# MHA decode with a ReGLU block: an eighth of the last query-weight row is loaded into the first 24 partitions by six short transfers

## The chip, the cores and the metric

One Trainium2 chip, one of its NeuronCores. The metric is the device time of one execution in microseconds (us). The core has 16 DMA engines that bring data from HBM into the on-chip memory of 128 partitions, and five compute engines: PE (TensorE), DVE (VectorE), ACT (ScalarE), POOL (GpSimd) and SP (SyncE, which here only issues transfers).

## What is computed

One token of a decoder layer. The reference, cut to what matters:

```python
def _A_ref(x, k_cache, v_cache, wq, wo):          # H, Dh = 32, 192; Sk = 8192; D = 640
    q = (x @ wq).reshape(B, Sq, H, Dh).transpose(0, 2, 1, 3)
    scores = jnp.einsum("bhqd,bhkd->bhqk", q, k_cache) * (Dh ** -0.5)
    p = _softmax(scores, axis=-1)
    o = jnp.einsum("bhqk,bhkd->bhqd", p, v_cache)
    return o.transpose(0, 2, 1, 3).reshape(B, Sq, H * Dh) @ wo

h  = x + _A_ref(_layernorm(x), k_cache, v_cache, wq, wo)
h2 = h + _B_ref(_layernorm(h), W_gate, W_up, W_down)   # (relu(gate) * up) @ W_down
```

All is in 32-bit floats. The two caches are 32 heads x 6 MB each; wq is 640 x 6144, which is 15 MB.

## The kernel before, in words

Everything large comes through one queue, the one that SP issues, and in the order of the program. A transfer of 128 rows fills one row in each partition.

**The query weights (L69 to L75).** Partition p holds the five rows 5p to 5p+4 of wq, 24 KB each. Three transfers bring them: rows 0 and 1 of each partition (6 MB, one tile of the pool `kv`), rows 2 and 3 (6 MB, the second tile), and row 4, the last (3 MB, half of the third tile). The pool `kv` has three such tiles and no more, so the loads of the caches take them over in turn: the first K load (head 0) waits until PE has done with rows 0 and 1, the second K load waits for rows 2 and 3, and the first V load for the last row.

**The queries (L154 to L164).** `xT` (x spread over the partitions, five values each) and `xrow` (x as one row) come on ACT's own queue, `xT` as 128 rows and `xrow` as a single row. After the layer norm, `xn` holds five normed values per partition, and for each j of 0 to 4 PE multiplies `xn[:, j]` with the weights' row j: 12 matmuls of 512 columns, three banks `qp0` to `qp2` by four groups of 32 output partitions. ACT copies the banks to `q4`, and `query(h)` (L168) spreads a pair of heads over all partitions.

**The heads (L292 to L310).** For each head SP loads K of the next head and V of this one, 6 MB each (48 KB a partition). DVE multiplies K by the query and sums (L188, L193) with POOL's help (L189), a softmax follows, and PE multiplies by V (L228). The rows of `wo` come in groups between them (L91).

**The end (L318 to L382).** The ReGLU weights take over two tiles of `kv`. Of W_down, twelve rows a partition, the last three come as transfers of one row each (L332), and the last four steps are: the last row of W_down lands, PE's last eight passes (L378), one DVE instruction (L381), the store of 640 results.

**Completion semaphores.** Each transfer adds to one of eight semaphores that the framework hands out in turn (DMAHW0 to DMAHW7 below). A transfer that is given a semaphore which an earlier transfer used waits on SP until that earlier one has landed.

The profile's line numbers are those of this listing.

Of the kernel before, what the change touches and what calls it, by code (L numbers as in the profile page):

```python
# [7 lines left out]
F32 = mybir.dt.float32  # L8
AF = mybir.ActivationFunctionType
ALU = mybir.AluOpType  # L10
AX = mybir.AxisListType
# [3 lines left out]
def kernel(  # L15
# [12 lines left out]
    nc = tc.nc  # L28
    P, Q, NQ = 128, 32, 4
    _, H, S, DH = kc.shape  # L30
    D = wq.shape[0]
    F = w_gate.shape[1]
    DJ = D // P
# [4 lines left out]
    TW = R * DH  # L38
    HPQ = H // NQ
    QB = 512  # L40
    NQB = HPQ * DH // QB
# [10 lines left out]
    const = ctx.enter_context(tc.tile_pool(name="const", bufs=1))  # L52
    kv = ctx.enter_context(tc.tile_pool(name="kv", bufs=3))
# [6 lines left out]
    ps_s = ctx.enter_context(tc.tile_pool(name="ps_s", bufs=2, space=bass.MemoryType.PSUM))  # L60
# [5 lines left out]
    nc.scalar.dma_start(xrow, x[0])  # L66


    wq_v = wq.rearrange("(p j) n -> p j n", p=P)  # L69
    wq_ts = []  # L70
    for j in range(0, DJ, 2):
        n = min(2, DJ - j)
        t3 = kv.tile([P, 2 * TW], F32, name="kv_t").rearrange("p (j n) -> p j n", n=TW)[:, 0:n, :]
        nc.sync.dma_start(t3, wq_v[:, j:j + n, :])
        wq_ts += [t3[:, i, :] for i in range(n)]  # L75

    def load_kv(src, h, parts):
        t = kv.tile([P, 2 * TW], F32, name="kv_t")
# [19 lines left out]
    ident = const.tile([P, P], F32, name="ident")  # L98
# [45 lines left out]
    xn = const.tile([P, DJ], F32, name="xn")  # L144
# [4 lines left out]
    for g in range(NQ):  # L149
        nc.tensor.matmul(acc[g * Q:(g + 1) * Q, :], ones[0:1, 0:Q], xrow[:, g * DG:(g + 1) * DG],  # L150
                         start=True, stop=False)


    qps = [ps_q.tile([P, QB], F32, tag="q", name=f"qp{b}") for b in range(2)]  # L154
    qps.append(ps_x.tile([P, QB], F32, tag="x", name="qp2"))
    for j in range(DJ):
        for b in range(NQB):
            for g in range(NQ):
                c0 = g * HPQ * DH + b * QB
                nc.tensor.matmul(qps[b][g * Q:(g + 1) * Q, :], xn[:, j:j + 1].to_broadcast([P, Q]),  # L160
                                 wq_ts[j][:, c0:c0 + QB], start=(j == 0), stop=(j == DJ - 1))
    q4 = const.tile([P, HPQ * DH], F32, name="q4")
    for b in range(NQB):
        nc.scalar.copy(q4[:, b * QB:(b + 1) * QB], qps[b])  # L164
# [129 lines left out]
    for h in range(H):  # L294
        gi, i = group_of[h]
# [80 lines left out]
    for j in range(FJ):  # L376
        for g in range(NQ):
            nc.tensor.matmul(pd[g * Q:(g + 1) * Q, 0:DG], guT[:, j, :], dn[:, j, g * DG:(g + 1) * DG],  # L378
                             start=(j == 0), stop=(j == FJ - 1))
# [30 lines left out]
```

## Time and profile before

| what | value |
|---|---|
| time, median of 3 runs | 1045.59 us (1045.57 to 1045.64) |
| time of the profiled execution | 1045.79 us |
| its span, first to last instruction | 1044.0 us |
| bytes moved in it | 446.35 MB, 428 GB/s over the span |
| busy: PE / DVE / POOL / ACT | 37% / 64% / 42% / 5% of the span |
| chain that ended last, by engine | DMA 62%, DVE 25%, PE 9%, issue 4% |

The span leaves out 1.8 us that lie around the instructions. "DMA share" in the rows below is the time that the packets which started in a stretch took, over 16 engines and the length of that stretch; it can exceed 1.00 by a little in a short stretch, since a packet counts where it started. One packet is one row of a transfer, or the word of 4 bytes that raises the semaphore. Engine busy times are in us, with the number of instructions in brackets.

### The profile page before, as it was taken

The numbers are of one execution on the slowest core, as the hardware profiler recorded it, in microseconds if no ns is written. First come the engines' busy times: TensorE is split into PE (matmuls) and PEld (weight loads), VectorE is DVE, ScalarE is ACT, GpSimd is POOL, SyncE is SP. The second block draws the span as 40 slices with busy tenths as digits, with TensorE's granted clock in tenths as the row PEclk, the third lists the DMA queues.
The fourth block names the chain that finished last, engine by engine and source line by source line (L and its number), as shares of the span: only waits on it lengthen the run. The fifth ranks groups of instructions, "written<-read, shape, count | busy, mean of one in ns | idle before, by whom it ended". The sixth has DMA issues, their size and how long they took to land.

```text
span 1044.0 us, 6866 instructions
## 1 busy us (share of the span) xinstructions
PE 391.3 (37%) x2872; PEld 126.6 (12%) x2872; DVE 666.6 (64%) x419; ACT 47.2 (5%) x141; POOL 440.2 (42%) x139
## 2 busy tenths in 40 slices
PE   1603343343345223344433333353323434341375
PEld 0101111011011011111110111011111111110122
DVE  1086777566667766567775666677665667766551
ACT  0000000000000000000000000000000000000010
POOL 0055555344455544245553444455542455544330
PEclk9856656666666566676656666665666666666678
DMA  9999999999999999999999999999999999999997
GB/s 396 441 427 431 430 439 430 429 430 441 424 432 433 436 426 428 440 434 429 434 432 432 429 436 433 432 428 436 433 420 443 434 430 431 432 432 427 433 422 297
DMA packets 13000, 446.35 MB, mean 428 GB/s; under 512 B 1573, under 2 KB 1577, under 8 KB 3114
## 3 DMA queue, kind: packets, MB, share of 16 engines
q1 hardware_dynamic: 12824, 445.92, 99.2%
q8 instruction: 22, 0.36, 0.1%
q14 instruction: 8, 0.07, 0.0%
q10 hardware_dynamic: 146, 0.01, 0.0%
HBM read 445.91 MB, written 0.00 MB: 427 GB/s over the span
## 4 chain that ended last, share of the span: by engine, by line
DMA 62%; DVE 25%; PE 9%; issue 4%; SPq 0%; ACTq 0%; ACT 0%; DVEq 0%
DMA kv_t<-in_A_k_cache_dram 57%; DVE kv_t L188 19%; PE po L228 6%; DVE sc L193 4%; DMA xrow<-in_A_x_dram 2%; DMA ffn_b<-in_B_W_down_dram 2%; DMA ffn_a<-in_B_W_up_dram 2%; PE q L173 2%; PE qp L160 1%; DVE oT L272 1%; DVE m L203 0%; DVE rl L213 0%; DVE mp L198 0%; SPq L82 0%; SPq L91 0%
## 5 line engine op out<-in xcount | busy, mean ns | idle before, releaser
L189 POOL TENSOR_TENSOR kv_t<-kv_t 128x1536 f32<-128x1536 f32 x128 | 438.3, 3447 | 559.8 <-DVE mp L198 254.6
L188 DVE TENSOR_TENSOR kv_t<-kv_t,q 128x3072 f32<-128x3072 f32 x128 | 427.5, 3343 | 300.6 <-DMA kv_t<-in_A_k_cache_dram 290.1
L228 PE MATMUL po<-kv_t,p 128*2 128x384 f32 x2048 | 215.3, 581 | 99.1 <-DMA kv_t<-in_A_v_cache_dram 99.0
L193 DVE TENSOR_REDUCE sc<-kv_t 128x16 f32<-128x1536 f32 x128 | 215.0, 1740 | 0.0
L200 PE MATMUL ps_small<-ident,mp 128*128 128x128 f32 x64 | 24.3, 483 | 399.3 <-DVE mp L198 399.3
L228 PEld LDWEIGHTS po<-kv_t,p 128*2 128x2 f32 x2048 | 53.7, 95 | 252.3 <-issue 147.9
L200 PEld LDWEIGHTS ps_small<-ident,mp 128*128 128x128 f32 x64 | 15.8, 307 | 421.3 <-issue 375.7
L268 PE MATMUL ps_small<-ob,par 128*32 128x192 f32 (+1 forms) x144 | 44.5, 479 | 0.7 <-ACT ob L231 0.7
L173 PE MATMUL q<-q,sel 128*128 128x384 f32 x32 | 21.3, 765 | 54.5 <-DVE kv_t L188 54.5
L231 ACT ACTIVATE ob<-po,rl 128x384 f32<-128x384 f32 x32 | 18.6, 581 | 437.9 <-PE po L228 437.9
L246 PE MATMUL acc<-wo_t,oT 128*3 128x480 f32 x112 | 32.9, 902 | 11.2 <-DVE oT L272 11.2
L210 PE MATMUL ps_small<-rs,ones 128*128 128x1 f32 x64 | 18.6, 359 | 48.1 <-ACT p L208 48.1
L205 ACT ACTIVATE nb<-m 128x1 f32<-128x1 f32 x32 | 6.5, 203 | 484.6 <-DVE m L203 484.4
L210 PEld LDWEIGHTS ps_small<-rs,ones 128*128 128x128 f32 x64 | 15.8, 308 | 74.6 <-ACT p L208 62.9
L268 PEld LDWEIGHTS ps_small<-ob,par 128*32 128x32 f32 x144 | 16.7, 154 | 16.1 <-issue 6.7
L160 PE MATMUL qp<-kv_t,xn 128*32 128x512 f32 x120 | 16.5, 705 | 3.9 <-DMA kv_t<-in_A_wq_dram 2.9
L272 DVE STREAM_TRANSPOSE oT<-ps_small 32x192 f32<-32x192 f32 (+1 forms) x32 | 11.6, 364 | 8.8 <-PE ps_small L268 8.1
L173 PEld LDWEIGHTS q<-q,sel 128*128 128x128 f32 x32 | 6.7, 258 | 63.8 <-DVE kv_t L188 49.6
L238 DVE MEMSET acc<- 128x512 f32 x1 | 0.5, 485 | 20.0 <-ACT q L164 20.0
L208 ACT ACTIVATE p<-sc,nb 128x64 f32<-128x64 f32 x32 | 11.2, 349 | 1.0
L127 DVE TENSOR_REDUCE s<-xT 128x1 f32<-128x5 f32 x1 | 0.2, 159 | 17.1 <-DMA xT<-in_A_x_dram 17.1
L203 DVE TENSOR_REDUCE m<-ps_small 128x1 f32<-128x128 f32 x32 | 9.1, 285 | 2.2 <-PE ps_small L200 2.2
(76 smaller groups left out, 76.5 us busy)
## 6 DMA issues: line engine op xcount, KB each, us to landing
kv_t<-in_A_k_cache_dram SPq DMA_DIRECT2D x32, 6144.0 KB, 37.0
kv_t<-in_A_v_cache_dram SPq DMA_DIRECT2D x31, 6144.0 KB, 23.1
wo_t<-in_A_wo_dram SPq DMA_DIRECT2D x7, 1920.0 KB, 27.0
kv_t<-in_A_wq_dram SPq DMA_DIRECT2D x2, 6144.0 KB, 18.1
ffn_a<-in_B_W_up_dram SPq DMA_DIRECT2D x1, 3840.0 KB
kv_t<-in_A_wq_dram SPq DMA_DIRECT2D x1, 3072.0 KB, 39.2
kv_t<-in_A_v_cache_dram SPq DMA_DIRECT2D x1, 3072.0 KB, 31.9
kv_t<-in_A_v_cache_dram SPq DMA_DIRECT2D x4, 768.0 KB, 35.5
```

The lines of the kernel that those rows point to most:

```text
L160: nc.tensor.matmul(qps[b][g * Q:(g + 1) * Q, :], xn[:, j:j + 1].to_broadcast([P, Q]), wq_ts[j][:, c0:c0 + QB], start=(j == 0), stop=(j == ...
L173: nc.tensor.matmul(q[:, 0:2 * DH], sel[:, g, :], q4[:, i * DH:(i + 2) * DH], start=True, stop=True)
L188: keep(nc.vector.tensor_mul(ks, ks, q[:, None, :].to_broadcast([P, SUB, DH])))
L189: nc.gpsimd.tensor_add(ks[:, :, 0:HD], ks[:, :, 0:HD], ks[:, :, HD:DH])
L193: keep(nc.vector.reduce_sum(sc[:, i0:i0 + SUB], ks[:, :, 0:HD], axis=AX.X))
L200: keep(nc.tensor.matmul(pt[:, 0:P], mp.to_broadcast([P, P]), ident, start=True, stop=True))
L210: nc.tensor.matmul(pl[:, 0:1], ones, rs, start=True, stop=True)
L228: nc.tensor.matmul(po[g * Q:g * Q + 2, :], p[:, 2 * i:2 * i + 2], vt[:, 2 * i * DH:(2 * i + 2) * DH], start=(i < NQ), stop=(i >= NP - NQ))
L231: nc.scalar.activation(ob, po, AF.Copy, scale=rl)
L246: nc.tensor.matmul(acc3[g * Q:g * Q + 3, 0:W3], oT[:, t:t + 3, 0], w3[:, g * W3:(g + 1) * W3], start=(gi == 0 and t == 0), stop=(gi == LAS ...
L268: nc.tensor.matmul(pt[q0:q0 + Q, 0:W], par[:, k, :], ob[:, k * DH + u * W:k * DH + (u + 1) * W], start=(k == 0), stop=(k == 1))
L272: keep(nc.vector.transpose(oT[s], pt[s, 0:W].rearrange("p (c j) -> p j c", c=Q)))
```

## The change

The last row of each partition is cut at column 5376. Its first 5376 columns come as before, in one transfer of 128 rows of 21 KB. The other 768 columns (3 KB), an eighth of the row, don't go to their own partition any more: the 128 pieces are put into the first 24 partitions, in six slots of 3 KB side by side. Slot s of 0 to 4 takes 24 pieces, those of the partitions 8s to 8s+7, 40+8s to 40+8s+7 and 80+8s to 80+8s+7; the last slot takes the eight pieces of the partitions 120 to 127. These six transfers stand ahead of that of the 5376 columns.

Since the pieces now lie in other partitions, the normed x values that belong to them must lie there too: `to_x` and `in_x` are two patterns of ones and zeros, made from the identity, and a matmul with them puts the 128 values of `xn[:, 4]` into `xx`, 24 partitions by six slots. PE then takes the 768 columns from the six slots: 12 matmuls with 24 (the last slot: 8) rows, added to the same banks.

```diff
     wq_ts = []
-    for j in range(0, DJ, 2):
-        n = min(2, DJ - j)
-        t3 = kv.tile([P, 2 * TW], F32, name="kv_t").rearrange("p (j n) -> p j n", n=TW)[:, 0:n, :]
-        nc.sync.dma_start(t3, wq_v[:, j:j + n, :])
-        wq_ts += [t3[:, i, :] for i in range(n)]
+    for j in range(0, DJ - 1, 2):
+        t3 = kv.tile([P, 2 * TW], F32, name="kv_t").rearrange("p (j n) -> p j n", n=TW)
+        nc.sync.dma_start(t3, wq_v[:, j:j + 2, :])
+        wq_ts += [t3[:, i, :] for i in range(2)]
+    t3 = kv.tile([P, 2 * TW], F32, name="kv_t")
+    wq_x = t3[:, TW:TW + SX * NX].rearrange("p (s n) -> p s n", n=NX)
+    wq_l = wq_v[:, DJ - 1, CX:TW]
+    wq_a = wq_l[0:5 * PX].rearrange("(a s b) n -> a b s n", a=3, b=8)
+    for s in range(SX - 1):
+        nc.sync.dma_start(wq_x[0:PX, s, :], wq_a[:, :, s, :])
+    nc.sync.dma_start(wq_x[0:8, SX - 1, :], wq_l[5 * PX:P])
+    nc.sync.dma_start(t3[:, 0:CX], wq_v[:, DJ - 1, 0:CX])
+    wq_ts.append(t3[:, 0:TW])
...
+    to_x = const.tile([P, PX], F32, name="to_x")
+    id_x = ident[:, 0:5 * PX]
+    nc.vector.reduce_sum(to_x.rearrange("p (a b) -> p a b", a=3), id_x.rearrange("p (a s b) -> p a b s", a=3, b=8),
+                         axis=AX.X)
+    nc.vector.tensor_add(to_x[:, 0:8], to_x[:, 0:8], ident[:, 5 * PX:P])
+    in_x = const.tile([P, SX], F32, name="in_x")
+    nc.vector.reduce_sum(in_x[:, 0:SX - 1], id_x.rearrange("p (a s b) -> p s a b", a=3, b=8), axis=AX.XY)
+    nc.vector.reduce_sum(in_x[:, SX - 1:SX], ident[:, 5 * PX:P], axis=AX.X)
+    xs = const.tile([P, SX], F32, name="xs")
+    nc.vector.tensor_scalar_mul(xs, in_x, xn[:, DJ - 1:DJ])
+    px = ps_s.tile([P, 512], F32, name="ps_small")
+    nc.tensor.matmul(px[0:PX, 0:SX], to_x, xs, start=True, stop=True)
+    xx = const.tile([PX, SX], F32, name="xx")
+    nc.vector.tensor_copy(xx, px[0:PX, 0:SX])
...
+    for s in range(SX):
+        k = PX if s < SX - 1 else 8
+        for b in range(NQB):
+            c1 = (NQ - 1) * HPQ * DH + (b + 1) * QB
+            c0 = max(c1 - QB, CX)
+            if c0 < c1:
+                query_part(b, NQ - 1, c0, c1, xx[0:k, s:s + 1].to_broadcast([k, Q]),
+                           wq_x[0:k, s, c0 - CX:c1 - CX], False, s == SX - 1)
```

Here CX = 5376, NX = 768, PX = 24 and SX = 6; `query_part` is the matmul of L160 with its columns given.

On SP's queue, at the program's start, the transfers stood so before (L74 the query weights, L82 the caches, L91 the rows of `wo`):

```order
L74 DMA kv_t<-in_A_wq_dram 128x12288 x2
L74 DMA kv_t<-in_A_wq_dram 128x6144
L82 DMA kv_t<-in_A_k_cache_dram 128x12288 [waits DMAHW1_49,PE_49]
L91 DMA wo_t<-in_A_wo_dram 128x3840
L82 DMA kv_t<-in_A_k_cache_dram 128x12288 [waits DMAHW3_49,PE_49]
L82 DMA kv_t<-in_A_v_cache_dram 128x12288 [waits DMAHW4_49,DMAHW0_49,PE_49]
```

and now so (L76, L83 to L85 the query weights, L93 the caches, L102 `wo`):

```order
L76 DMA kv_t<-in_A_wq_dram 128x12288 x2
L83 DMA kv_t<-in_A_wq_dram 24x1x768 x4
L83 DMA kv_t<-in_A_wq_dram 24x1x768 [waits DMAHW0_49]
L84 DMA kv_t<-in_A_wq_dram 8x768 [waits DMAHW1_49]
L85 DMA kv_t<-in_A_wq_dram 128x5376 [waits DMAHW2_49]
L93 DMA kv_t<-in_A_k_cache_dram 128x12288 [waits DMAHW3_49,PE_49]
L102 DMA wo_t<-in_A_wo_dram 128x3840 [waits DMAHW4_49]
L93 DMA kv_t<-in_A_k_cache_dram 128x12288 [waits DMAHW5_49,PE_49]
```

There are four transfers more, and the eight semaphores now go round once within the query weights: the fifth short transfer waits for `xT` (DMAHW0), the sixth for rows 0 and 1 of the weights (DMAHW1), the long rest for `xrow` (DMAHW2), and the first K load for rows 2 and 3 (DMAHW3).

On PE, the matmuls of the weights' last row stood so before (`qp_149` to `qp_151` are the three banks):

```order
L160 MATMUL qp_149<-kv_t,xn 32x512 [waits DMAHW4_49]
L160 MATMUL qp_149<-kv_t,xn 32x512 x3
L160 MATMUL qp_150<-kv_t,xn 32x512 x4
L160 MATMUL qp_151<-kv_t,xn 32x512 x4
L173 MATMUL q<-q_212,sel 128x384 [waits Activation_49,Pool_49]
```

and now so:

```order
L185 MATMUL qp_167<-kv_t,xn 32x512 [waits DMAHW2_49]
L185 MATMUL qp_167<-kv_t,xn 32x512 x3
L185 MATMUL qp_168<-kv_t,xn 32x512 x3
L185 MATMUL qp_168<-kv_t,xn 32x256
L185 MATMUL qp_169<-kv_t,xn 32x512 x3
L185 MATMUL qp_168<-kv_t,xx 32x256 [waits DMAHW4_49,DVE_49]
L185 MATMUL qp_169<-kv_t,xx 32x512
L185 MATMUL qp_168<-kv_t,xx 32x256 [waits DMAHW5_49]
```

The twelve matmuls became 11 and then six pairs (two pairs' beginnings are shown), each pair waiting for its own short transfer. The matmul with `to_x` (L176) stands ahead of the first matmul of the weights.

## Rows read from the trace of the kernel before

**Rows 1.** the page's part 3: queue, kind: packets, MB, share of 16 engines' span
```profile
q1 hardware_dynamic: 12824, 445.92, 99.2%
q8 instruction: 22, 0.36, 0.1%
```

**Rows 2.** busy time by stretch: engines, granted PE clock, DMA share, GB/s
```profile
60.00:400.00 340.00, 121.61 (x832) 38.35 (x832) 241.29 (x138) 14.77 (x45) 163.31 (x48) 0.62 1.00 432
400.00:1000.00 600.00, 219.17 (x1544) 70.58 (x1548) 407.96 (x238) 24.50 (x80) 273.31 (x80) 0.63 1.00 431
```

**Rows 3.** the chain that ended last, 1000 to 1044: start us, us, what
```profile
1021.66 18.58 DMA ffn_b<-in_B_W_down_dram
1040.28 0.52 PE pd L378 x8
1040.83 0.38 DVE o L381
```

**Rows 4.** busy time by stretch, the last 7 us of the transfers
```profile
1033.00:1034.00 1.00, 0.00 (x0) 0.00 (x0) 0.94 (x2) 0.00 (x0) 0.00 (x0) 1.00 1.01 405
1034.00:1034.50 0.50, 0.47 (x16) 0.45 (x20) 0.00 (x0) 0.00 (x0) 0.00 (x0) 1.00 0.96 389
1034.50:1035.00 0.50, 0.50 (x18) 0.22 (x8) 0.00 (x0) 0.00 (x0) 0.00 (x0) 1.00 0.65 266
1035.50:1036.00 0.50, 0.46 (x16) 0.44 (x20) 0.00 (x0) 0.00 (x0) 0.00 (x0) 1.00 0.53 215
1037.00:1038.00 1.00, 0.13 (x4) 0.13 (x8) 0.00 (x0) 0.00 (x0) 0.00 (x0) 1.00 0.52 202
1039.00:1039.50 0.50, 0.18 (x10) 0.01 (x2) 0.00 (x0) 0.00 (x0) 0.00 (x0) 1.00 0.12 46
1039.70:1039.90 0.20, 0.20 (x8) 0.00 (x0) 0.00 (x0) 0.00 (x0) 0.00 (x0) 1.00 0.04 13
```

**Rows 5.** DMA packets that start between 1.7 and 3.1 us
```profile
DMA packets 16, 0.79 MB, mean 562 GB/s; under 512 B 0, under 2 KB 0, under 8 KB 0
```

**Rows 6.** queue 10's packets in 18.4 to 18.5, 18.98 to 19, 20.89 to 20.9
```profile
q10 hardware_dynamic: 2, 0.00, 1.1%
...
q10 hardware_dynamic: 1, 0.00, 31.9%
...
q10 hardware_dynamic: 1, 0.00, 5.6%
```

**Rows 7.** DMA packets that start between 115.6 and 115.7 us, by queue
```profile
q8 instruction: 1, 0.02, 68.4%
```

**Rows 8.** DMA issues (KB each, median us to landing), then the timeline (start us, us)
```profile
ffn_b<-in_B_W_down_dram SPq DMA_DIRECT2D x3, 320.0 KB, 27.5
...
1039.49 0.48 PE L378 MATMUL pd<-ffn_b,guT 128*32 128x160 f32 x8 [0.32 <-DMA ffn_b<-in_B_W_down_dram]
1040.28 0.48 PE L378 MATMUL pd<-ffn_b,guT 128*32 128x160 f32 x8 [0.31 <-DMA ffn_b<-in_B_W_down_dram]
```

**Rows 9.** timeline of the front: start us, us, what [idle before <-releaser]
```profile
19.03 0.16 DVE L127 TENSOR_REDUCE s<-xT 128x1 f32<-128x5 f32 x1 [17.15 <-DMA xT<-in_A_x_dram]
21.33 0.74 PE L150 MATMUL acc<-xrow,ones 1*32 1x160 f32 x2 [1.50 <-DMA xrow<-in_A_x_dram]
31.02 0.33 SPq L82 DMA_DIRECT2D kv_t<-in_A_k_cache_dram  x1
33.41 7.05 PE L160 MATMUL qp<-kv_t,xn 128*32 128x512 f32 x48 [2.46 <-DMA kv_t<-in_A_wq_dram]
40.94 2.78 PE L160 MATMUL qp<-kv_t,xn 128*32 128x512 f32 x24 [0.48 <-DMA kv_t<-in_A_wq_dram]
43.78 0.33 SPq L82 DMA_DIRECT2D kv_t<-in_A_v_cache_dram  x1
55.58 13.15 DVE L188 TENSOR_TENSOR kv_t<-kv_t,q 128x3072 f32<-128x3072 f32 x4 [10.54 <-DMA kv_t<-in_A_k_cache_dram]
```

**Rows 10.** all 68 cache loads (L82): issue to landing
```profile
DMA to landing us min/median/max: 22.8/33.4/45.3
```

More of the change, by code (lines that the diff above doesn't have):

```diff
@@ L69 @@
     wq_v = wq.rearrange("(p j) n -> p j n", p=P)
+    CX, NX, PX, SX = TW - 768, 768, 24, 6
     wq_ts = []
-    for j in range(0, DJ, 2):
-        n = min(2, DJ - j)
-        t3 = kv.tile([P, 2 * TW], F32, name="kv_t").rearrange("p (j n) -> p j n", n=TW)[:, 0:n, :]
-        nc.sync.dma_start(t3, wq_v[:, j:j + n, :])
-        wq_ts += [t3[:, i, :] for i in range(n)]
+    for j in range(0, DJ - 1, 2):
[11 more added lines that the diff above has]
+    wq_ts.append(t3[:, 0:TW])
     def load_kv(src, h, parts):
@@ L151, with query_part @@
                          start=True, stop=False)
+    to_x = const.tile([P, PX], F32, name="to_x")
[12 more added lines that the diff above has]
+    nc.vector.tensor_copy(xx, px[0:PX, 0:SX])
     qps = [ps_q.tile([P, QB], F32, tag="q", name=f"qp{b}") for b in range(2)]
     qps.append(ps_x.tile([P, QB], F32, tag="x", name="qp2"))
+    def query_part(b, g, c0, c1, lhs, w, start, stop):
+        d = g * HPQ * DH + b * QB
+        nc.tensor.matmul(qps[b][g * Q:(g + 1) * Q, c0 - d:c1 - d], lhs, w, start=start, stop=stop)
     for j in range(DJ):
@@ L159 @@
                 c0 = g * HPQ * DH + b * QB
-                nc.tensor.matmul(qps[b][g * Q:(g + 1) * Q, :], xn[:, j:j + 1].to_broadcast([P, Q]),
-                                 wq_ts[j][:, c0:c0 + QB], start=(j == 0), stop=(j == DJ - 1))
+                c1 = c0 + QB
+                last = j == DJ - 1
+                moved = last and c1 > CX
+                if moved:
+                    c1 = max(c0, CX)
+                if c0 < c1:
+                    query_part(b, g, c0, c1, xn[:, j:j + 1].to_broadcast([P, Q]), wq_ts[j][:, c0:c1],
+                               j == 0, last and not moved)
+    for s in range(SX):
[3 more added lines that the diff above has]
+            c0 = max(c1 - QB, CX)
+            if c0 < c1:
+                query_part(b, NQ - 1, c0, c1, xx[0:k, s:s + 1].to_broadcast([k, Q]),
+                           wq_x[0:k, s, c0 - CX:c1 - CX], False, s == SX - 1)
     q4 = const.tile([P, HPQ * DH], F32, name="q4")
```

## The prediction, made before the changed kernel ran

> **What bounds the kernel now.** I read the queues first, then the stretches, then the chain's end, then the last microseconds one half at a time.
>
> SP's queue holds nearly all the bytes, and its packets fill 99.2% of 16 engines' span [rows 1]. In the two long stretches that hold 940 us the DMA share is 1.00, at 431 to 432 GB/s [rows 2]. So the 16 engines never wait for an issue there, and one engine moves 432 / 16 = 27.0 GB/s. Compute runs beside this; what waits for DMA in the middle is not what to shorten. The chain's end says the same: the last landing of W_down, then 0.52 us of PE, then 0.38 us of DVE, and the store [rows 3]. The time ends when the slowest engine has moved its share.
>
> The engines don't finish together [rows 4]. Until 1034 the share is 1.01. These last rows have packets of 2.5 KB, at which a busy engine shows about 0.95 of its time, so the share times 16 / 0.95 counts the engines still at work: 11 from 1034.5 to 1035 (0.65), 9 from 1035.5 on (0.53 and, two us later, 0.52), 2 from 1039 (0.12), and less than one from 1039.7 (0.04). Five engines stop near 1034.4, two more near 1035.3, nine go on, and the last one stops near 1039.8. So seven engines are ahead of the last: five by some 5.4 us, two by some 4.5 us. Bytes moved from the late engines to those seven shorten the kernel; bytes moved the other way lengthen it.
>
> What makes engines unequal is seen in part. A packet of the instruction queue took 0.684 x 0.1 x 16 = 1.09 us of one engine [rows 7], and there are 22 [rows 1]; dealt to nine engines that is 2.7 us each, near the gap between the two groups.
>
> **What the change moves.** Each 128-row transfer puts eight rows on each engine: the first 16 packets are one row of 48 KB for each of 16 engines (0.79 MB) [rows 5]. The change takes 3 KB from each of 128 rows, on every engine 8 x 3,072 = 24,576 bytes, which at 27.0 GB/s is **-0.91 us on each of the 16**.
>
> What it adds depends on how 24 rows are dealt, which no row shows. The ends are: even over all 16 (0.91 us come back, nothing moved) and all on one engine (128 packets there). The nearest rows are the 128-row transfers with eight rows an engine, so I take eight an engine: 24 rows are three engines, in five transfers, and the last eight rows fall one to an engine on eight. An engine of the three gets 5 x 8 + 1 = 41 packets of 3 KB. Price of one: the 2.5 KB rows of W_down land 0.79 us apart for a 320 KB transfer [rows 8], eight packets an engine, so 0.099 us each, and by size 0.119 us for 3 KB. That is 41 x 0.119 = 4.9 us, and net **+4.0 us on three engines**; five others get one packet, **-0.8 us**; eight keep **-0.91 us**. With all 128 on one engine it would be 128 x 0.119 - 0.91 = +14.3 us there.
>
> [...]
>
> Which three? A single row goes to one engine, and `xrow` was that: its packet started at 18.98 to 19.00, its semaphore word at 20.89 to 20.90 [rows 6], one 48 KB packet (1.82 us at 27.0 GB/s) behind it. So its engine had ended its part of `xT` at 18.98 - 1.82 = 17.2, while the last engine did so between 18.4 and 18.5 [rows 6]. I take a short transfer to begin on that same engine: it is 1.3 us ahead at the start. Its two neighbours are not seen. If all three are among the five that lead by 5.4 us, they end 1.4 us ahead of the old end, the late ones 0.91 ahead, and the gain is full. If one is among the two with 4.5 us, it ends 0.5 ahead, and that is the gain.
>
> **What else it touches, and what covers it.** SP's fifth short transfer waits for `xT` (19.03), the sixth for rows 0 and 1, the rest for `xrow` (21.3) [rows 9]. Rows 2 and 3 are in the queue until 33.4 [rows 9], so 12 us cover these waits. The first K load moves from 31.02 to some 33.5 (it now waits for rows 2 and 3); the rest still in the queue is 8 x 21,504 bytes an engine, 6.4 us, which covers it. The six small DVE instructions and one matmul stand ahead of PE's first weights: at 0.16 us [rows 9] to 0.25 us each, at most 2 us, before a wait that ends at 33.41 anyway. PE's last row was 24 passes in 2.78 us [rows 9], 0.116 each; now it is 46, at most 5.3 us, and begins up to 4 us later: the first V load moves from 43.78 to 50 at most, with two loads and `wo` ahead of it (33 us of queue). Queries are ready near 51, K lands at 55.5 [rows 9] or up to 3 us later on the loaded engines. Then buffers come free 3 us later; the shortest load took 22.8 us from issue to landing [rows 10], and itself needs 6,144 KB / 432 GB/s = 14.6 us, so 8 us of older work stood before it. All nothing on the path; if the cover failed, the loss would be what an engine idles.
>
> **Sum.** -0.91 us at the late engines, the three loaded ones just below: -0.3 to -0.91, and I take -0.8. The profiled execution, 1045.79 us, would give 1045.0; its span of 1044.0 and the 1.8 us around it otherwise stay. It lies 0.2 us over the median 1045.59, so I forecast **1044.8 us**, range of this case 1044.6 to 1045.3. That is under 0.1%, and 0.2% (2.1 us) is about what a measurement of this kernel can tell from no change.
>
> **Rivals.**
> - *One of the three is a late engine.* The nine late ones lead the last by 0 to some 2.5 us, since nine are still at work after 1037 [rows 4]. With +4.0 us on it the end moves by +1.5 to +4.0 us: 1047.1 to 1049.6, **slower**. It decides when a loaded engine leads the last by less than 4.0 us. For it: nine of 16 are late, and only one of the three is seen, only at the start. Against it: that one is ahead, and the late group is explained by instruction packets, which I would expect to be dealt to a fixed part of the engines, more likely a run of neighbours than a scatter. Chance 0.15.
> - *The 24 rows are spread over more engines.* Then nothing is moved and 41 small packets become 8 to 11 an engine: 8 x 0.119 - 0.91 = +0.04 us, **1045.6 us**. [...] For it: 128 rows do so; against: 24 is no multiple of 16. Chance 0.06.
> - *The front runs dry* through the new waits on SP. The loads then start late and every engine idles alike; up to 1 us, **1046.3 us**. The 12 and 6.4 us of cover speak against it. Chance 0.03.
> - *Faster by over 0.2%* needs 2.1 us, more than the 0.91 us that leave a late engine; only another dealing of instruction packets could add it. Chance 0.02.
>
> The forecast keeps 0.74. Within 0.2% lie the forecast, the spread, most of the dry front and the mildest of the late engine: 0.84. Slower by over 0.2%: 0.13. Faster: 0.03. For eight in ten the range must hold the forecast, the spread and the dry front: 1044.4 to 1046.4 us, 0.83.
>
> **What would show it.** In the changed profile: the queue's packets grow by 128 rows and 23 semaphore words (three for each of five transfers, eight for the sixth); in the last microseconds fewer engines stop at 1034, since three of the seven now go on to about 1038.5, and the last stops near 1038.9; the share stays 1.00 in the long stretches. Wrong would be: a share that falls to one or two engines for several us at the end (a late engine was loaded), or seven engines that still stop at 1033.5 (nothing was moved).

## The result, and the profile after

The changed kernel took **1050.82 us** (median of six runs, 1048.17 to 1051.55), beside 1045.62 us (1045.41 to 1045.9) for the kernel before on the same chip: ratio 1.0043, 95% interval 1.003 to 1.0056. It is slower by 5.2 us, outside the range that was given. The profiled execution took 1050.48 us, with a span of 1048.6 us. Four of the six runs took 1050.5 to 1051.6 us and two 1048.2 and 1048.4; what is read below is a profile of the first kind, and no view tells why two runs were spared some 2.5 us, which is about what the late query is found to cost below.

The queues come first: the page's part 3 of the changed kernel, to be laid beside [rows 1].

```profile
q1 hardware_dynamic: 12975, 445.92, 99.1%
q8 instruction: 23, 0.38, 0.1%
```

The bytes are the same, and SP's queue has 151 packets more: 128 short rows and 23 semaphore words, which is three for each of five transfers and eight for the sixth. Of the 146 packets on ACT's queue 129 are the rows of `xT` and `xrow` and 17 such words, one of them for the single row of `xrow` [rows 6] and so 16 for the 128 rows of `xT`; three words are then three engines. The 24 rows were dealt as predicted, and the fault is not there.

Next the stretches. This is the busy time by stretch in the front of the changed kernel, with the columns of [rows 2]; DMA share and GB/s are the last two.

```profile
32.00:34.00 2.00, 1.12 (x12) 0.29 (x12) 0.00 (x0) 0.00 (x0) 0.00 (x0) 1.00 1.07 330
34.00:36.00 2.00, 2.00 (x24) 0.65 (x20) 0.00 (x0) 0.00 (x0) 0.00 (x0) 1.00 1.09 296
36.00:38.00 2.00, 2.00 (x24) 0.52 (x16) 0.00 (x0) 0.00 (x0) 0.00 (x0) 1.00 0.84 230
38.00:40.00 2.00, 0.48 (x8) 0.00 (x0) 0.00 (x0) 0.00 (x0) 0.00 (x0) 1.00 1.08 328
40.00:42.00 2.00, 0.00 (x0) 0.00 (x0) 0.00 (x0) 0.00 (x0) 0.00 (x0) 0.98 1.09 467
```

Read the last two columns together. The share stays near 1.0, so the engines are busy; yet they move 230 to 330 GB/s where the long stretches have 432 [rows 2]. A packet simply takes longer: the trace's rows of 21.5 KB that started from 34 to 38 us took 1.13 to 1.42 us each, those from 42 us on 0.80 to 0.81. The stretch is the one in which the short transfers are in flight, and at 40 us, when they are done, the rate is back.

The timeline of the front, to be laid beside [rows 9]:

```profile
33.16 0.33 SPq L93 DMA_DIRECT2D kv_t<-in_A_k_cache_dram  x1
...
46.64 5.34 PE L185 MATMUL qp<-kv_t,xn 128*32 128x512 f32 x22 [8.16 <-DMA kv_t<-in_A_wq_dram]
...
51.91 12.21 PE L185 MATMUL qp<-kv_t,xx 24*32 24x256 f32 x24
...
64.14 0.33 SPq L93 DMA_DIRECT2D kv_t<-in_A_v_cache_dram  x1
...
65.73 13.15 DVE L233 TENSOR_TENSOR kv_t<-kv_t,q 128x3072 f32<-128x3072 f32 x4 [0.33 <-PE q L218]
```

PE waits 8.16 us for the last row, which lands at 46.6 and not at 40.9. Then come the 24 passes on the short rows: 12.21 us, 0.51 us each. They are not alike, since the 768 columns of a slot fall into a piece of 256 and one of 512; the groups of instructions from 46 to 66 us, forms kept apart, show it for the first five slots (busy us, then mean ns of one):

```profile
L185 PE MATMUL qp<-kv_t,xx 24*32 24x512 f32 x10 | 7.2, 811 | 0.0
L185 PE MATMUL qp<-kv_t,xx 24*32 24x256 f32 x10 | 4.0, 489 | 0.0
```

The first V load is issued at 64.14 (43.78 before), and what releases DVE is now the query (PE q) and no longer K's landing; it starts at 65.73 in place of 55.58.

What that late start does is seen 35 us further on, again by stretch:

```profile
100.00:104.00 4.00, 4.00 (x30) 0.88 (x32) 4.00 (x4) 0.00 (x0) 2.56 (x1) 0.58 0.74 319
104.00:106.00 2.00, 2.00 (x32) 0.58 (x28) 1.60 (x1) 0.00 (x0) 0.00 (x0) 1.00 0.20 82
106.00:107.00 1.00, 1.00 (x20) 0.19 (x8) 0.00 (x0) 0.00 (x0) 0.00 (x0) 1.00 2.38 688
107.00:108.00 1.00, 0.32 (x4) 0.00 (x0) 0.00 (x0) 0.58 (x1) 0.00 (x0) 1.00 0.27 98
108.00:109.00 1.00, 0.00 (x0) 0.00 (x0) 0.00 (x0) 0.00 (x0) 0.00 (x0) 1.00 0.34 147
```

(A packet is counted in the stretch in which it starts, hence 2.38.) The queue is nearly empty from 104 to 106 us: the next V load goes out only at 105.63 us, when DVE has freed a buffer. Over these nine us the engines fall behind 432 GB/s by (432 - 319) x 4 + (432 - 82) x 2 + (432 - 688) + (432 - 98) + (432 - 147) = 1,515 GB/s x us, which is 3.5 us of their work. Before, the same place was full (a share of 0.91 to 1.08 from 100 to 108 us, 393 GB/s or more), and from 400 to 1000 us the rate is the old one, 432 GB/s; nothing is made up.

The chain's end, as in [rows 3]:

```profile
1026.33 18.52 DMA ffn_b<-in_B_W_down_dram
1044.84 0.04 issue
1044.89 0.52 PE pd L423 x8
```

W_down lands 4.6 us later than before (1040.24); the 18.5 us it takes and the 0.9 us behind it are the old ones. And the last stretches, as in [rows 4]:

```profile
1040.00:1041.00 1.00, 0.79 (x24) 0.68 (x24) 0.00 (x0) 0.00 (x0) 0.00 (x0) 1.00 0.73 300
1042.00:1043.00 1.00, 0.49 (x16) 0.47 (x20) 0.00 (x0) 0.00 (x0) 0.00 (x0) 1.00 0.54 215
1043.00:1044.00 1.00, 0.80 (x24) 0.39 (x16) 0.00 (x0) 0.00 (x0) 0.00 (x0) 1.00 0.35 141
1044.00:1045.00 1.00, 0.59 (x12) 0.27 (x16) 0.00 (x0) 0.00 (x0) 0.00 (x0) 1.00 0.11 34
```

No group of seven stops early, as one did in [rows 4], and no one or two engines work on alone for several us: the engines end one after another over some 5 us.

So there are two suspects, the slow stretch at 32 to 40 us and the late query with the empty queue. Fourteen further kernels tell them apart. They ran on several chips, and each is set beside the kernel before on its own chip.

### The profile page after: what moved, and what is told of

It is laid out like the page before. It is cut to its first block, busy times and chain, and to the rows that moved or that the text cites. A ratio compares the mean times of both kernels' runs of the same rounds, so it can differ in the third digit from the quotient of the medians.

```text
span 1048.6 us, 6928 instructions
## 1 busy us (share of the span) xinstructions
PE 408.1 (39%) x2896; PEld 131.1 (13%) x2896; DVE 667.6 (64%) x425; ACT 47.1 (4%) x141; POOL 440.0 (42%) x139
## 4 chain that ended last, share of the span: by engine, by line
DMA 61%; DVE 24%; PE 10%; issue 4%; SPq 0%; ACTq 0%; DVEq 0%
DMA kv_t<-in_A_k_cache_dram 54%; DVE kv_t L233 19%; PE po L273 7%; DVE sc L238 4%; DMA kv_t<-in_A_wq_dram 2%; DMA xrow<-in_A_x_dram 2%; PE q L218 2%; DMA ffn_b<-in_B_W_down_dram 2%; DMA ffn_a<-in_B_W_up_dram 2%; PE qp L185 2%; DVE oT L317 1%; DVE m L248 0%; DVE rl L258 0%; DVE mp L243 0%; SPq L93 0%
## 5 line engine op out<-in xcount | busy, mean ns | idle before, releaser
L273 PE MATMUL po<-kv_t,p 128*2 128x384 f32 x2048 | 217.7, 587 | 98.3 <-DMA kv_t<-in_A_v_cache_dram 98.3
L185 PE MATMUL qp<-kv_t,xn 128*32 128x512 f32 (+1 forms) x118 | 17.4, 724 | 9.0 <-DMA kv_t<-in_A_wq_dram 9.0
L185 PE MATMUL qp<-kv_t,xx 24*32 24x256 f32 (+3 forms) x24 | 12.2, 682 | 0.0
```

The costliest lines, as they stand in the source:

```text
L185: nc.tensor.matmul(qps[b][g * Q:(g + 1) * Q, c0 - d:c1 - d], lhs, w, start=start, stop=stop)
L273: nc.tensor.matmul(po[g * Q:g * Q + 2, :], p[:, 2 * i:2 * i + 2], vt[:, 2 * i * DH:(2 * i + 2) * DH], start=(i < NQ), stop=(i >= NP - NQ))
```

## The experiments

### The late query, and what it costs alone

**Short matmuls first** (the edit is to the changed kernel: the twelve short matmuls stand ahead of the last row's, since their rows land first).

```diff
     for j in range(DJ):
+        if j == DJ - 1:
+            for s in range(SX):
...
+                        query_part(b, NQ - 1, c0, c1, xx[0:k, s:s + 1].to_broadcast([k, Q]),
...
-    for s in range(SX):
...
```

> The twelve short matmuls stand ahead of the weights' last row on PE, so they run while PE waits for that row (38.5 to 46.6 us in the changed kernel's trace). Late query: the query of head 0 is ready some 10 us earlier (near 55 instead of 65.7), the first K load (61.2) ends the wait again, the second V load is issued near 101 instead of 105.6, and the queue hardly runs empty: 1047.3 us (1046.3 to 1048.0), that is 3 us below the change; what is left over the kernel before is the slowed front. Loaded engine: the order on PE changes nothing at the end, 1050.5 us.

Measured: 1048.21 us beside 1045.73 before, ratio 1.0024 (1.0015 to 1.0034). The timeline's rows on PE and SP:

```profile
38.95 10.02 PE L185 MATMUL qp<-kv_t,xx 24*32 24x256 f32 x24
...
48.90 5.34 PE L185 MATMUL qp<-kv_t,xn 128*32 128x512 f32 x22
...
54.29 0.33 SPq L93 DMA_DIRECT2D kv_t<-in_A_v_cache_dram  x1
```

V's load is issued 10 us earlier than in the changed kernel, DVE again waits for K (61.13 us), and no stretch between 100 and 108 us is under 393 GB/s. Half of the loss is gone by the order of PE's work alone; 2.5 us stay.

**No short matmuls** (the changed kernel without them).

```diff
-    for s in range(SX):
-        k = PX if s < SX - 1 else 8
...
-                query_part(b, NQ - 1, c0, c1, xx[0:k, s:s + 1].to_broadcast([k, Q]),
-                           wq_x[0:k, s, c0 - CX:c1 - CX], False, s == SX - 1)
...
```

> Left out: the twelve short matmuls, so the last row's part of 768 columns is missing from the queries; the six short transfers stay. Late query: query ready near 53, no empty queue near 105, 1047.2 us (1046.2 to 1048.0). Loaded engine: the bytes are where they were, 1050.5 us.

Measured: 1048.22 us beside 1045.73 before, ratio 1.0025 (1.0015 to 1.0035), the same as with the short matmuls first. So these cost nothing where they stand early, and where they stand last 5.20 - 2.49 = 2.7 us, each kernel against the one before on its chip. The front is still slow, and the end is better balanced than before:

```profile
34.00:36.00 2.00, 2.00 (x20) 0.67 (x24) 0.00 (x0) 0.00 (x0) 0.00 (x0) 1.00 0.96 264
36.00:38.00 2.00, 2.00 (x24) 0.64 (x20) 0.00 (x0) 0.00 (x0) 0.00 (x0) 1.00 0.97 264
...
1037.00:1038.00 1.00, 0.70 (x23) 0.36 (x12) 0.00 (x0) 0.00 (x0) 0.00 (x0) 1.00 0.74 305
1039.00:1040.00 1.00, 0.21 (x8) 0.00 (x0) 0.00 (x0) 0.00 (x0) 0.00 (x0) 1.00 0.70 279
```

Five and three us before its end some 12 engines are at work (0.74 and 0.70 x 16 / 0.95), where the kernel before had nine [rows 4]. That is what it would be if three of the seven early engines took the bytes; no view names an engine. The balance that the prediction was about seems to be there, under a loss of another kind; a table below comes back to it.

**Late query alone** (the kernel before, with idle copies on ACT ahead of the query's use).

```diff
+    for i in range(28):
+        nc.scalar.copy(q4[:, 0:QB], qps[0])
```

> The kernel before, with 28 repeated copies on ACT that hold the first query back by some 20 us; no transfer is changed. Late query: DVE starts on K of head 0 near 65 instead of 55.6, the second V load is issued near 105 instead of 95.5, the queue is empty for 3 to 5 us there, and the time is 1049.5 us (1048 to 1051). Loaded engine or slowed transfers: no byte is moved, 1045.6 us.

Measured: 1048.55 us (1047.49 to 1049.76), ratio 1.0026 (1.0016 to 1.0037). The front is at its old rate, DVE starts at 62.48 us behind PE's query, and the queue runs empty near 100 us:

```profile
100.00:102.00 2.00, 2.00 (x24) 0.50 (x20) 2.00 (x2) 0.00 (x0) 0.00 (x0) 0.78 0.52 221
```

A query that is late by 7 us (62.48 in place of 55.58) costs 2.8 us in a kernel whose transfers are untouched. That is shown, then: the late query is a loss of its own, of about the size that is missing between 1048.2 and 1050.8, though its own eight runs are spread over 2.3 us.

### What makes the transfers slow

**Two parts of 128 rows** (the kernel before; its last row comes as 768 and 5,376 columns, all 128 partitions each).

```diff
+        if n == 1:
+            nc.sync.dma_start(t3[:, :, TW - 768:TW], wq_v[:, j:j + 1, TW - 768:TW])
+            nc.sync.dma_start(t3[:, :, 0:TW - 768], wq_v[:, j:j + 1, 0:TW - 768])
...
```

> The kernel before, with the last row of the weights in two transfers of 128 rows, 768 columns and then 5376; nothing moves to another engine or partition. Late query and loaded engine: 1045.6 us, and the packets of 21 KB take 0.80 us each. If packets of 3 KB or 21 KB are slow by their size alone (1.2 us for 21 KB, as in the changed kernel between 33 and 40 us): 1047.5 us or more.

Measured: 1045.86 us, ratio 1.0 (0.9991 to 1.0009), and 429 GB/s at 34 to 38 us. So packets of 3 KB and of 21.5 KB are not slow by their size.

Then four variations of the kernel without short matmuls, each with one thing changed in the short transfers:

```diff
# another source: contiguous pieces of W_up
-    wq_l = wq_v[:, DJ - 1, CX:TW]
+    wq_l = w_up.rearrange("d (t n) -> (d t) n", n=NX)[0:P]
# other partitions
-        nc.sync.dma_start(wq_x[0:PX, s, :], wq_a[:, :, s, :])
+        nc.sync.dma_start(wq_x[64:64 + PX, s, :], wq_a[:, :, s, :])
...
# behind the 5,376 columns
+    nc.sync.dma_start(t3[:, 0:CX], wq_v[:, DJ - 1, 0:CX])
     for s in range(SX - 1):
...
-    nc.sync.dma_start(t3[:, 0:CX], wq_v[:, DJ - 1, 0:CX])
# rows in one run
-        nc.sync.dma_start(wq_x[0:PX, s, :], wq_a[:, :, s, :])
+        nc.sync.dma_start(wq_x[0:PX, s, :], wq_l[s * PX:(s + 1) * PX])
```

> As e2 (the twelve short matmuls left out), but the short transfers read 128 pieces of 3 KB that lie side by side in W_up, in place of the last row's pieces, so wrong columns are loaded, to the same 24 partitions by the same three engines. If the slowed stretch (264 to 298 GB/s from 32 to 38 us in e2) comes from where the pieces lie in HBM: 430 GB/s in that stretch and 1045.0 us (1044.6 to 1045.6). If from the partitions they go to, or from three engines with short packets: 280 GB/s and 1048.2 us as in e2.

> As e2, but the short transfers go to partitions 64 to 87 in place of 0 to 23. Same three engines, same source. If the slowed stretch comes from engines that write into partitions 0 to 23 beside the engines whose rows those are: the stretch changes, and if it goes 1045.0 us. If from the source or from the short packets on three engines: 280 GB/s and 1048.2 us as in e2.

> As e2, but the short transfers stand behind the 5376 columns in the queue, beside the first K load. If the slowing belongs to short packets on three engines whatever runs beside them: the 5376 columns move at 430 GB/s until about 38 us, the slow stretch moves to 38 to 47 us, and the time stays near 1048.2 us. If it needs the same rows of the weights beside them: no slow stretch, 1045.0 us.

> [...] If three engines with short packets are the cause: no slow stretch, and 1045.5 us, with seven engines early at the end as before the change. If the destination is the cause: a slow stretch of 2 to 3 us at least and 1046.5 us or more.

Measured, beside 1045.88 us before: another source 1048.43 us, ratio 1.0025 (1.0015 to 1.0036); other partitions 1048.58, 1.0026 (1.0016 to 1.0036); behind the columns 1048.32, 1.0023 (1.0013 to 1.0032); rows in one run 1047.72, 1.0017 (1.0008 to 1.0027). The source is out, and so is the mere position of the 24 partitions. With the short transfers behind the columns the slow stretch moves with them, and it now catches K's packets:

```profile
34.00:38.00 4.00, 4.00 (x40) 1.30 (x36) 0.00 (x0) 0.00 (x0) 0.00 (x0) 1.00 1.04 439
...
42.00:44.00 2.00, 2.00 (x13) 0.74 (x7) 0.21 (x1) 1.17 (x2) 0.00 (x0) 1.00 1.00 272
```

With rows in one run more engines share 24 rows (the queue has 45 packets more than in the changed kernel, which is 12 semaphore words for each of five transfers in place of three), and the stretch is shorter and as deep (234 GB/s at 32 to 34 us, 409 at 36 to 38). So it isn't that three engines are overloaded either. What may be common to all of these is that rows of the short transfers go to partitions that, in a 128-row transfer, another engine writes. Call such a partition foreign to the engine that writes it. No view shows which engine writes which partition, so this is a conjecture.

**Own partitions, foreign partitions, and two halves** test it. The first two are built on the kernel without short matmuls, the third on the kernel before. The short rows go to partitions 0 to 11 and 32 to 43 in the first and to 80 to 91 and 112 to 123 in the second; the first pair was taken for the engines' own, the second for foreign ones, and the two halves for a mixture. No run shows that, and the names of the kernels say no more than which partitions they use.

```diff
# own partitions; foreign ones: (80, 112) in place of (0, 32)
+    for s in range(3):
+        for p0 in (0, 32):
+            nc.sync.dma_start(wq_x[p0:p0 + 12, s, :], wq_a[:, :, 2 * s + p0 % 64 // 32, :])
...
# two halves
-        nc.sync.dma_start(t3, wq_v[:, j:j + n, :])
+        if n == 1:
+            for p0 in (0, P // 2):
+                nc.sync.dma_start(t3[p0:p0 + P // 2], wq_v[p0:p0 + P // 2, j:j + n, :])
...
```

> As the version without the twelve short matmuls (it leaves the moved eighth of the last row out of the product), but the six short transfers are of 12 rows of 5 KB each: three to partitions 0 to 11 and three to partitions 32 to 43, four rows for each of three engines in a transfer. [...] Theory A, an engine that writes partitions of another engine slows all of them: the packets of 21.5 KB take about 0.80 us as in a 128-row transfer, the stretch 32 to 40 us moves about 430 GB/s, and the time is 1044.8 to 1045.8 us. Theory B, any transfer that uses only three engines slows all sixteen while it is in flight: 32 to 40 us at 230 to 310 GB/s and about 1048.2 us, as without the short matmuls.

> [...] Theories A (foreign partitions) and B (fewer than sixteen engines) both say about 1048.2 us and 230 to 310 GB/s between 32 and 40 us. A third theory, that it was the six rows of 3 KB in one partition or the strided rows, says 1045 us here too.

> The kernel before with its last row of the query weights in two transfers of 64 rows, to partitions 0 to 63 and then 64 to 127, of 24 KB each. [...] Theory A (foreign partitions): the packets of 24 KB take 1.2 us or more where such a row took 0.91 us, a stretch of some 7 to 12 us between 30 and 42 us falls under 350 GB/s, and the time is 1047 to 1049 us. Theory B (fewer than sixteen engines): nothing changes, 1045.4 to 1046.0 us.

Measured, beside 1045.77 us before: **own partitions 1044.88 us** (ten runs, 1044.72 to 1045.13; before, 14 runs, 1045.67 to 1046.5), ratio 0.999 (0.9981 to 1.0); **foreign partitions 1049.68 us**, 1.0036 (1.0022 to 1.005); **two halves 1054.14 us**, 1.0079 (1.0064 to 1.0094). The busy time by stretch, 34 to 38 us, of the kernel with own partitions:

```profile
34.00:38.00 4.00, 4.00 (x40) 1.17 (x36) 0.00 (x0) 0.00 (x0) 0.00 (x0) 1.00 1.05 447
```

The same stretch with foreign partitions:

```profile
34.00:38.00 4.00, 3.73 (x36) 1.19 (x40) 0.00 (x0) 0.00 (x0) 0.00 (x0) 1.00 1.13 237
```

And with two halves:

```profile
34.00:38.00 4.00, 4.00 (x24) 1.15 (x28) 0.00 (x0) 0.00 (x0) 0.00 (x0) 0.57 0.97 197
```

The first two kernels differ in two numbers, the partitions, and by 4.8 us. The third has no short row, keeps all 16 engines busy (share 0.97) and still falls to 197 GB/s, where the kernel before moves 416: it moves 128 x 24,576 bytes = 3.15 MB so, 16.0 us in place of 7.3, and loses 8.4. Theory B (fewer than 16 engines) is out by both ends, and that the partitions to which the short rows go decide is shown. Whether they do because an engine writes those of another is not. Theory A had the sign and not the size: it gave foreign partitions about 1048.2 us and two halves 1047 to 1049.

The packets show how many engines are slow. With own partitions 127 of the 128 rows of 21.5 KB took 0.80 to 0.81 us. With foreign ones 52 such rows started from 34 to 40 us, and each took 1.61 to 1.64 us. An engine that takes one row after another at 1.6 us each starts at most four in 6 us, so these 52 lie on 13 engines at least; the short rows took 0.40 us in place of 0.20, and the 30 of them that started from 34 to 38 us (12 us of work in 4) fill three more. All 16 go at half their rate. In two halves the rows of 24 KB that started from 34 us on took 1.66 to 2.06 us, where before they took 0.91.

Why all 16 engines are slow when three of them write the short rows is not shown. If only those three were slow, and three more whose partitions they write, ten would go on at 432 / 16 = 27 GB/s, 270 together; all 16 show 237. No run here explains it.

The ends tell the balance from the slow front. This is the DMA share in each of the last six us before W_down's last landing:

| kernel | landing at | share, us by us | sum |
|---|---|---|---|
| before | 1040.24 | 0.68 0.57 0.54 0.50 0.20 0.05 | 2.54 |
| two halves | 1048.39 | 0.70 0.58 0.55 0.48 0.23 0.04 | 2.58 |
| own partitions | 1039.40 | 0.94 0.73 0.73 0.62 0.31 0.04 | 3.37 |

Two halves loads the same rows into the same partitions as the kernel before, and after its slow front it ends as that does (2.58 beside 2.54). Own partitions gets 0.8 us more work out of the 16 engines in these six us, and is 0.89 us faster. So the more even end comes from the bytes that were moved.

### Both cures in a whole kernel

A whole kernel that keeps the pieces of 3 KB to such partitions has transfers of 12 or 16 rows here, so more of them. **Whole, four engines** puts the moved eighth on partitions 0 to 15 and 32 to 47 in eight transfers, multiplies both kinds in one matmul of 48 rows with zeros between, and runs a quarter of the short matmuls early. **Early zeros** has these zeros written by GpSimd, and **three engines** goes back to 12 rows, in ten transfers and one of eight rows.

```diff
+    nc.vector.memset(t3[0:32, TW:TW + SX * NX], 0.0)
+    wq_a = wq_v[:, DJ - 1, CX:TW].rearrange("(i a s b) n -> i s a b n", i=2, a=4, b=4)
...
+            nc.sync.dma_start(wq_x[32 * i:32 * i + 16, s, :], wq_a[i, s])
...
+        if last:
+            short([0], False)
...
+    short([1, 2, 3], True)
# early zeros
-    nc.vector.memset(t3[0:32, TW:TW + SX * NX], 0.0)
+    nc.gpsimd.memset(t3[0:32, TW:TW + SX * NX], 0.0)
# three engines
-            nc.sync.dma_start(wq_x[32 * i:32 * i + 16, s, :], wq_a[i, s])
+            nc.sync.dma_start(wq_x[32 * i:32 * i + 12, s, :],
+                              wq_h[i, 0:60].rearrange("(a s b) n -> s a b n", a=3, b=4)[s])
```

> A whole version that follows from the runs to own partitions: the moved eighth goes to partitions 0 to 15 and 32 to 47 in eight transfers of 16 rows of 3 KB (four rows for each of four engines), the two kinds of partitions are multiplied together (48 rows, of which 16 hold zeros), and a quarter of the short matmuls runs ahead of the last row's. Every engine has 8 packets of 3 KB less and four have 32 more: 0.95 us less on twelve engines, 2.85 us more on four. If foreign partitions were what slowed the transfers and the order of PE's work what made the query late, both losses are gone: 32 to 40 us at some 430 GB/s, V0's load issued before 57 us, no stretch between 96 and 108 us under 350 GB/s, and 1044.7 to 1045.2 us where before has 1045.75. If four engines with 2.85 us more hold one that was late, 1046.5 to 1047.5. If something else in the changed kernel costs, 1047 or more.

Measured: 1048.64 us beside 1045.74 before, ratio 1.0028 (1.0017 to 1.0038). The zeros stood behind DVE's work on the norm and were written at 26 us; SP, which waited for them, issued the first short transfer at 29.11 and the last row at 32.65, and the queue ran low at 30 to 34 us (share 0.59, 207 GB/s). That is a new wait that this version made, and the run says nothing on the theory.

> The whole version to partitions 0 to 15 and 32 to 47 once more, with the zeros between them written by GpSimd, which has nothing to do from about 6 us to the first scores, and no longer by DVE, which came to them at 26 us. SP then issues the first short transfers before 20 us and the last row before 24 us. If foreign partitions and the late query were the whole loss: no stretch between 26 and 44 us at under 380 GB/s over 4 us, V0's load issued before 54 us, 1044.6 to 1045.3 us where before has 1045.75. If one of the four loaded engines was a late one: 1045.8 to 1047.5 with a full queue in the front. If a third cause costs, over 1047 with a full queue in the front and no late engine at the end.

Measured: 1048.05 us beside 1045.64 before, ratio 1.0025 (1.0014 to 1.0036). Both cures hold in its front: 437 GB/s at 34 to 38 us, 432 from 26 to 60 us (434 before), V's load at 48.12, no stretch under 393 at 98 to 108. But its end is this:

```profile
1038.00:1039.00 1.00, 0.59 (x20) 0.26 (x8) 0.00 (x0) 0.00 (x0) 0.00 (x0) 1.00 0.44 169
1039.00:1040.00 1.00, 0.11 (x4) 0.11 (x8) 0.00 (x0) 0.00 (x0) 0.00 (x0) 1.00 0.15 59
1040.00:1041.00 1.00, 1.00 (x20) 0.85 (x23) 0.00 (x0) 0.00 (x0) 0.00 (x0) 0.54 0.06 23
1041.00:1042.00 1.00, 1.00 (x24) 0.81 (x19) 0.00 (x0) 0.00 (x0) 0.00 (x0) 0.50 0.05 20
```

A share of 0.06 is one engine of 16, and it works on alone for some 2 us. That is the sign which the prediction gave for its rival of a loaded late engine, here with four engines in place of three.

> The whole version with early zeros, but to partitions 0 to 11 and 32 to 43: ten transfers of 12 rows and one of 8 rows of 3 KB, so that three engines take what four took: 36, 36 and 32 packets of 3 KB more than before on them (4.3, 4.3 and 3.8 us by 0.119 us each), 0.95 us less on the thirteen others. If the lone engine at the end of the version before was the fourth, loaded though late, the ends have no share of 0.06 or less for over 1 us, and the time is 1044.6 to 1045.3 us where before has 1045.7. If one of the first three is late as well, or if a third cause costs, 1047 us or more.

Measured: 1047.0 us (1046.49 to 1047.61) beside 1045.77 before, ratio 1.0011 (1.0002 to 1.002). Nearer, but not under the kernel before. The lone engine is gone; two or three are left at the end:

```profile
1040.00:1041.00 1.00, 1.00 (x20) 0.72 (x20) 0.00 (x0) 0.00 (x0) 0.00 (x0) 0.55 0.16 61
1041.00:1042.00 1.00, 0.94 (x28) 0.42 (x20) 0.00 (x0) 0.00 (x0) 0.00 (x0) 1.00 0.13 37
```

Eleven short transfers also keep SP waiting: K's first load goes out at 36.94 and `wo` at 41.82 (31.02 and 31.39 before), and the first scores start at 59.22 us, 1.25 us later than with own partitions in six transfers (57.97). The stretch from 26 to 60 us, three engines and then the kernel before:

```profile
26.00:60.00 34.00, 25.28 (x147) 6.80 (x146) 1.42 (x3) 1.75 (x3) 0.00 (x0) 0.92 1.00 420
26.00:60.00 34.00, 16.27 (x120) 4.35 (x112) 4.91 (x3) 1.76 (x3) 0.93 (x1) 0.77 1.01 434
```

14 GB/s less over 34 us is 1.1 us of the engines' work, about what this version is behind the kernel before. So the gain of the balance, 0.9 us, is missing as well; which engines end last here, and whether they are the loaded three, is left open. None of the three whole versions beats the kernel before.

## Why the prediction was wrong

**The bound** was read rightly: share 1.00 in the long stretches (429 and 432 GB/s from 60 to 1000 us in the changed kernel too), and a time set by the slowest engine.

**How 24 rows are dealt** was right: three engines, 151 packets more.

**The balance** was right too, and its size, in the one kernel that shows it alone: own partitions gained 1045.77 - 1044.88 = 0.89 us, and the term was -0.91 at the late engines and -0.8 in the sum. The ten runs lie apart from those of the kernel before, though the interval of the ratio, 0.9981 to 1.0, reaches up to no change. This kernel leaves out the short matmuls and moves 24.6 KB less, which is 0.06 us. The first three engines were early enough in that run; that this holds in other kernels isn't shown, and three engines speaks against it.

**The price of a moved packet** was the first step that failed: "by size 0.119 us for 3 KB. That is 41 x 0.119 = 4.9 us". It took the rate that the 128-row transfers have by themselves for that of the 24-row transfers and of what runs beside them, and took it that 13 engines go on untouched. All 16 slowed, to 230 to 330 GB/s together for 8 us. The packets of 21.5 KB took 1.13 to 1.42 us in the slow stretch, where 0.80 was taken for granted. The cost is the step from own partitions to no short matmuls: each against its own kernel before, +2.49 and -0.89, so 3.4 us. The rates agree: from 30 to 42 us the kernel without short matmuls moved 304, 264 and 380 GB/s in stretches of 4 us, the kernel before 393, 416 and 473; 1,336 GB/s x us less, over 432, is 3.1 us. No row of before shows a transfer of fewer than 128 rows beside others, and the bounds on this price were taken on how the rows are dealt, and none on the rate.

**The cover in the front** was the second: "0.116 each; now it is 46, at most 5.3 us". The 0.116 us is from passes that take turns over four groups of output partitions. The 24 short passes all lie on one group, one behind another, and took 0.51 us each, 12.21 us. The 22 others took 5.34 us. The profile has the difference: of these 22 a pass of 512 columns took 1,061 ns on the mean while one came every 0.24 us, so some four ran at a time; on the one group it took 811 ns, and one came every 0.72 us (7.2 us for ten). The granted clock (before the last two columns) has a part in it: it was 0.50 when the row came, after PE had waited 8.16 us; at 1.00, below, 22 such passes took 2.77 us.

```profile
46.00:52.00 6.00, 5.36 (x23) 1.07 (x24) 0.00 (x0) 0.59 (x1) 0.00 (x0) 0.50 1.00 434
52.00:64.00 12.00, 12.00 (x24) 3.13 (x24) 0.00 (x0) 0.59 (x1) 0.00 (x0) 0.64 1.00 429
```

At a clock of 1.00 the timeline of early zeros has the same two kinds of passes, the short ones again half of 256 and half of 512 columns:

```profile
41.33 2.77 PE L185 MATMUL qp<-kv_t,xn 128*32 128x512 f32 x22 [1.17 <-DMA kv_t<-in_A_wq_dram]
44.03 4.05 PE L185 MATMUL qp<-kv_t,xx 48*32 48x256 f32 x12
```

That is 0.34 us for a short pass of 384 columns on the mean, where the price taken was 0.116 us for one of 512: three times as much by the pass, and nearly four times by the column. The row itself landed 5.7 us later and not "up to 4". So the first V load went out at 64.14 where "50 at most" stood, queries came at 65.7 where "near 51" stood, and "All nothing on the path" fell. DVE began 10.2 us later. For some 3 us of that the transfers were late as well, so the queue had that much more left to do; late query alone shows that the other 7 are more than it covers, where "8 us of older work" were counted on. That step costs 5.2 - 2.49 = 2.7 us; alone, in the kernel before, 2.8.

The three add up: -0.89 + 3.38 + 2.71 = 5.2 us. They are steps from one kernel to the next, so the exact sum is built in. What bears it out is that late query alone costs as much, 2.8, and the bytes of the changed kernel's two bad stretches, of which the first stands beside the kernel before above (434 GB/s; from 95 to 115 us it had 433):

```profile
26.00:60.00 34.00, 24.96 (x137) 6.73 (x130) 0.00 (x0) 0.59 (x1) 0.00 (x0) 0.78 1.01 402
95.00:115.00 20.00, 10.32 (x73) 3.19 (x72) 16.26 (x10) 0.58 (x1) 9.73 (x4) 0.67 0.89 365
```

That is 32 GB/s less over 34 us and 68 less over 20, 2.5 and 3.1 us of the engines' work. Less the 0.9 of the balance it makes 4.8, and the two profiled executions differ by 1050.48 - 1045.79 = 4.7. So the whole is sound, and the parting between the two losses is uncertain by nearly 1 us.

**The rivals.** "The front runs dry" had nearest the place, a stretch in which all engines idle alike, but put it down to SP's waits and bounded it by 1 us; the waits on SP did cost nothing in the changed kernel (share 0.98 at 26 to 32 us). The change did not meet the late engine; the end of the version with four engines looks like it. Spreading was out, since three engines took the rows. So the rivals covered how bytes are dealt, and no rival had the rate or PE's order in it; the range of 2 us was built from those rivals, and missed by 4.4.

## What to carry to other kernels

Before you move bytes between DMA engines, ask to which partitions they will go: the gain here was 0.9 us with partitions 0 to 11 and 32 to 43 (in a kernel without the product of the moved bytes; no whole one kept it), and the loss 1.8 to 3.9 us with the others that were tried (0 to 23, 64 to 87, 80 to 91 and 112 to 123), with nearly the same bytes. Don't price a transfer of fewer than 128 rows beside full ones by its bytes alone (here they moved 447 GB/s together in one case and 237 in another); look at the GB/s of the stretch at a share of 1.0, which tells slow packets from missing ones. And price added matmuls by the group of output partitions on which they lie: passes that all lie on one group cost nearly four times as much by the column here (0.34 us for 384 columns, 0.116 for 512), and where they stand in PE's order decided here whether 12 us were free or cost 2.7.

## What the runs showed of the hardware that was not expected

- Two transfers of 64 rows, to the two halves of the partitions, moved 197 GB/s with all 16 engines busy (share 0.97); the one of 128 rows moved 416 in the same stretch. Splitting one row of the weights so cost 8.4 us of 1046.
- Short rows to partitions 80 to 91 and 112 to 123 slowed all 16 engines: 237 GB/s, beside 447 in the same stretch with partitions 0 to 11 and 32 to 43, and 1.61 to 1.64 us for a row of 21.5 KB, beside 0.80.
- Passes of 48 rows, half by 256 and half by 512 columns, on a single group of 32 output partitions took 0.34 us each at a clock of 1.00; those of 512 columns that take turns over four groups took 0.12.
- What the slow stretch and the empty queue lost by 115 us was not made up in the 900 us that followed, at a share of 1.00: W_down landed 4.6 us later than before.
